# First loads of a fused attention and FFN kernel in 2 KB rows, split by partitions, with a third centred tile and a new hand-written order

## The chip, the cores and the metric

The kernel runs on one core of a Trainium2 chip. The metric is the device time of one execution in microseconds (us), the median of several runs. A core has five engines that run at the same time: TensorE (PE) for matrix products, VectorE (DVE), ScalarE (ACT), GpSimd (POOL) and SyncE (SP). SP and ACT also issue the transfers (DMAs) between the main memory and the on-chip memory. Each engine works through its own queue in order and waits at semaphores for the others.

## The reference

The input is x with 2048 tokens of 512 numbers in bf16. It is normalised per token, and two branches read the normalised xn; both are added to x.

```python
def reference(A_x, A_wqkv, A_wo, B_x, B_w_gate, B_w_up, B_w_down):
    xn = _layernorm(A_x)                       # eps 1e-5, no weights
    # A: linear attention, 32 heads of 16, over all tokens (no mask)
    q, k, v = split(xn @ A_wqkv)
    phi = lambda t: jnp.where(t > 0, t + 1, jnp.exp(t)) + 1e-6
    kv  = jnp.einsum("bhsd,bhse->bhde", phi(k), v)
    z   = jnp.einsum("bhsd->bhd", phi(k))
    o   = (phi(q) @ kv) / (phi(q) @ z + 1e-6)
    # B: gated FFN, 1792 wide
    return A_x + o @ A_wo + (silu(xn @ B_w_gate) * (xn @ B_w_up)) @ B_w_down
```

The sums over tokens in kv and z do not depend on the order of the tokens.

## The kernel before, in words

The 2048 tokens are 16 tiles of 128 tokens (tokens on the 128 partitions). The program is recorded by `_Program`: each step names its engine, what it reads and what it writes, and the class places the semaphores. The order in which steps are recorded is the order of every engine's queue; nothing is scheduled at run time. For the first part that order is written out by hand as a text of words in `run("""...""")`, one letter for the step and a number for the tile. `U0` and `U1` are the first two blocks of the FFN; a loop records the rest behind them.

The letters that matter here, with the lines of the profile before:

- `S` statistics of a tile on DVE: `bn1` (L257) and `bn2` (L263); tile 0 in two halves, `bnhalf` (L260) and `stat0`. `R` is `rs` on ACT (L272, L274): reciprocal standard deviation by Ln and Exp; `r` adds three powers of it (L279 to L281).
- `L` (`lna_dve`, L335) and `P` (`lna_pool`, L350 and L353) write the normalised tile xn on DVE or POOL.
- A centred tile goes another way: only the mean is subtracted before the projections, and the standard deviation is put in later as a scale inside Exp (L421) and as limits (`o`, `floor`, L284 and L287). `a` and `b` centre the halves of tile 0 (L297); `M` is the negative mean on ACT (`neg_mean`, L292) and `C` centring with it (L307); `J` (`xg_pool`, L327 and L330) writes the scaled tile that the sums over tokens need. The tiles in `CENTRED` are 0 and 1. Their xn is written later for the FFN alone.
- `c`, `d`, `W`, `X` are transposes on PE (`transp`, L365) of tiles 0 to 3; `e`, `g`, `h`, `v`, `w`, `Y` copy the result out of PSUM on ACT (L373) or DVE (L375). All other transposes are `D`, DMA transposes from SP (L381).
- `K` and `Q` are the projections of a tile (`proj`, L403), four products of 128x512 over the four chunks of the weight; `K0:3` is chunk 3 alone. `x` and `y` are their Exp on ACT (`phi_exp`, L421 centred, L424 otherwise), `m` and `n` the limits on POOL (`phi_min`, L431), `s` and `u` the sums on DVE (`phi_sum`, L442), which also free the PSUM banks. `G` (`gacc`, L452) adds a tile into the sums over tokens; these use banks 0 to 3, the projections mostly banks 4 to 7 in turn.
- `F1` is a filler product of 256 columns on PE (`keep_busy`, L247); seven of 512 columns stand ahead of all.
- `l` is a load of a later x tile from SP; `T0` to `T7` are the large weight loads from SP (0 and 4 the gate halves, 1 and 5 the up halves, 2 the value weights, 3 `wo`, 6 and 7 `wd`).

The first loads stand ahead of the text, on two queues: `("sp", "h00 K0 Q0 Q3 Q2 K1")` and `("act", "h01 x2 x3 Q1 x1 K3 K2")`. `h00` and `h01` are the column halves of x tile 0; each `K` or `Q` word is one 128x512 chunk of the weight, in rows of 1 KB.

The FFN (`gu`, L508; `hop`, L521), the output products (L638, L642) and the stores (L648 to L651) follow. `z_add`, `divide` and `scale_turn` compute the denominators beside them.

Of the kernel before, what the change touches and what calls it, by code (L numbers as in the profile page):

```python
# [9 lines left out]
P = 128  # L10
S = 2048
D = 512
F = 1792
NT = S // P
NCH = S // 512
NG = D // P
NDC = D // P
# [3 lines left out]
HPG = P // DH  # L21
NH = D // DH

CENTRED = (0, 1)
NC = len(CENTRED)
HALVED = (0,)
LOWBANK = {(1, 2): 0, (0, 2): 1}
NWARM = 7
O_SLOT = {5: 0, 8: 1, 11: 2, 13: 3}
# [79 lines left out]


def bass_parallel_sum__linear_attn_block__swiglu_ffn__prompt_kernel(nc, A_x, A_wqkv, A_wo, B_x, B_w_gate, B_w_up, B_w_down, out):
    xin = A_x[0]
    oview = out[0]
    K = _Program()
    bf, f32 = dt.bfloat16, dt.float32

    with contextlib.ExitStack() as es:
# [5 lines left out]
        x_sb = sb("x_sb", [P, NT, D], bf)  # L123
        xn = sb("xn", [P, NT, D], bf)
        r2 = sb("r2", [P, NC], f32)
# [7 lines left out]
        wqkv = sb("wqkv", [P, NDC, 3 * D], bf)  # L133
# [18 lines left out]
        out_sb = sb("out_sb", [P, 2, D], bf)  # L152
# [6 lines left out]
        stats = sb("stats", [P, NT + 1, 6], f32)  # L159
        mv = sb("mv", [P, NT, 2], f32)  # L160
# [7 lines left out]
        zt = pz[:, 0, :]  # L168
        shared = {(1, t): [("xc", t, 0), ("xc", t, 1)] for t in CENTRED}
        shared.update({(1, NC + t): [("xg", t)] for t in CENTRED})  # L170
        shared.update({(1, 2 * NC + a): [("xcT", t, h) for t in CENTRED for h in (0, 1)] for a in CENTRED})
        shared[1, 3 * NC] = [("junk",)]
# [5 lines left out]
        def B(i):  # L178
            return ("bank", i)


        def load(eng, key, dst, src):
            K.add(eng, lambda e: e.dma_start(dst, src), w=[key], dma=True)

        def xload(eng, t):
            load(eng, ("x", t), x_sb[:, t, :], xin[t * P:(t + 1) * P, :])

        def wload(eng, i, h=0, n=1):
            cs = slice(h * NDC // n, (h + 1) * NDC // n)
# [19 lines left out]
        K.add("act", lambda e: e.preload_act_table_set("natural_log_exp_and_others"))  # L209
        H = D // 2  # L210

        def xhalf(eng, t, h):
            load(eng, ("x", t, h), x_sb[:, t, h * H:(h + 1) * H], xin[t * P:(t + 1) * P, h * H:(h + 1) * H])

        def wchunk(eng, i, c):
            load(eng, ("wqk", i, c), wqkv[:, c, i * D:(i + 1) * D], A_wqkv[c * P:(c + 1) * P, i * D:(i + 1) * D])

        for eng, text in (("sp", "h00 K0 Q0 Q3 Q2 K1"),
                          ("act", "h01 x2 x3 Q1 x1 K3 K2")):
            for w in text.split():  # L220
                if w[0] == "h":
                    xhalf(eng, int(w[1:-1]), int(w[-1]))
                elif w[0] == "x":
                    xload(eng, int(w[1:]))
                else:
                    wchunk(eng, int(w[0] == "K"), int(w[1:]))

        K.add("pool", lambda e: e.memset(eps5[:, :], 1e-5), w=[("eps5",)])
        K.add("pool", lambda e: e.memset(ident[:, :], 0.0), w=[("ident",)])
# [1 line left out]
            out=ident[:, :], in_=ident[:, :], compare_op=ALU.not_equal, fill=1.0,  # L231
# [24 lines left out]
        def bn1(t):  # L256
            K.add("dve", lambda e: e.bn_stats(stats[:, t, :], x_sb[:, t, :]), r=xk(t), w=[("st", t)])  # L257

        def bnhalf(h):
            K.add("dve", lambda e: e.bn_stats(stats[:, h * NT, :], x_sb[:, 0, h * H:(h + 1) * H]), r=[("x", 0, h)], w=[("st", h * NT)])  # L260

        def bn2(t):
            K.add("dve", lambda e: e.bn_aggr(mv[:, t, :], stats[:, t, :]), r=[("st", t)], w=[("mv", t)])  # L263

        def stat0():
            bnhalf(0)
            bnhalf(1)
            K.add("dve", lambda e: e.bn_aggr(mv[:, 0, :], stats[:, 0::NT, :]), r=[("st", 0), ("st", NT)], w=[("mv", 0)])

        def rs(t):  # L270
            sl = slice(t, t + 1)
# [105 lines left out]
        def xkeys(t):  # L377
            return [("xnT", t)]
# [14 lines left out]
        def proj(i, t, cs):  # L393
            if (i, t) not in at:
                at[i, t] = LOWBANK[i, t] if (i, t) in LOWBANK else nextbank()
                begun[i, t] = 0
            b, col = at[i, t], i * D
            src = xcT if t in CENTRED else xnT
            fns = []
            for c in cs:  # L400
                first, last = begun[i, t] == 0, begun[i, t] == NDC - 1
                begun[i, t] += 1
                fns.append(lambda e, c=c, first=first, last=last: e.matmul(  # L403
                    banks[b][:, :], src[:, c, t * P:(t + 1) * P], wqkv[:, c, col:col + D], start=first, stop=last))
            keys = sorted({("xcT", t, c // 2) for c in cs}) if t in CENTRED else xkeys(t)
            K.add("pe", fns, r=keys + [("wqk", i, c) for c in cs], w=[B(b)])

        def efslot(b):
            return b - 4 if b >= 4 else b + 4
# [5 lines left out]
        def phi_exp(i, t):  # L415
            b = at[i, t]
            buf, bkey = ef[:, efslot(b), :], ("ef", efslot(b))
            if i == 0 and t in later:
                buf, bkey = pq[:, t, :], ("pq", t)
            if t in CENTRED:  # L420
                K.add("act", lambda e: e.activation(buf, banks[b][:, :], ACT.Exp, bias=lstd[:, t:t + 1], scale=rstd[:, t:t + 1]),  # L421
                      r=[B(b), ("rs", t), ("lstd", t)], w=[bkey])
            else:
                K.add("act", lambda e: e.activation(buf, banks[b][:, :], ACT.Exp), r=[B(b)], w=[bkey])  # L424

        def phi_min(i, t):
            buf, bkey = ef[:, efslot(at[i, t]), :], ("ef", efslot(at[i, t]))
            if i == 0 and t in later:
                buf, bkey = pq[:, t, :], ("pq", t)
            top, tkeys = (cap[:, t:t + 1], [("cap", t)]) if t in CENTRED else (1.0 + 1e-6, [])  # L430
            K.add("pool", lambda e: e.tensor_scalar(  # L431
                out=buf, in0=buf, scalar1=top, scalar2=0.0, op0=ALU.min, op1=ALU.max),
                r=[bkey] + tkeys, w=[bkey])

        def phi_sum(i, t):
            b = at[i, t]
            dst, dkey = ((pk[:, t, :], ("pk", t)) if i else (pq[:, t, :], ("pq", t)))
            low, lkeys = (flo[:, t:t + 1], [("flo", t)]) if t in CENTRED else (1e-6, [])
            val, mid, keys = banks[b][:, :], ef[:, efslot(b), :], [B(b), ("ef", efslot(b))]
            if i == 0 and t in later:  # L440
                val, mid, keys = tq[later[t]], pq[:, t, :], [("tq", later[t]), ("pq", t)]
            K.add("dve", lambda e: e.scalar_tensor_tensor(  # L442
                out=dst, in0=val, scalar=low, in1=mid, op0=ALU.max, op1=ALU.add),
                r=keys + lkeys, w=[dkey])
# [31 lines left out]
                  r=[fkey, ("pk", t)], w=[key])  # L476

        def stat(t):
            if t == 0:
                stat0()  # L480
                return
            bn1(t)
            bn2(t)

# [6 lines left out]
            "h": lambda t: evac(t, 2 * t + 1, "act", 2, 4), "f": lambda t: evac(t, 2 * t + 1, "dve", 2, 4),  # L491
            "W": lambda t: transp(t, 2), "v": lambda t: evac(t, 2, "act"), "w": lambda t: evac(t, 2, "dve"),
            "X": lambda t: transp(t, 3), "Y": lambda t: evac(t, 3, "act"), "Z": lambda t: evac(t, 3, "dve"),
            "l": lambda t: xload("sp", t), "K": lambda t, cs=range(NDC): proj(1, t, cs), "x": lambda t: phi_exp(1, t), "m": lambda t: phi_min(1, t), "s": lambda t: phi_sum(1, t),
            "Q": lambda t, cs=range(NDC): proj(0, t, cs), "y": lambda t: phi_exp(0, t), "z": phi_keep, "n": lambda t: phi_min(0, t), "u": lambda t: phi_sum(0, t), "G": gacc, "F": lambda t: keep_busy(t, 256),
        }

# [40 lines left out]
        def run(text):  # L538
# [5 lines left out]
                steps[k](t) if cs is None else steps[k](t, cs)  # L544

        run("""
            F1 F1 F1 S0 a0 R0 l9 c0 F1 r0 l13 F1 S2 J0 F1 g0 F1 b0 Q0:0 d0 R2 K0:0 h0 F1 o0 L2 W2 Q0:3 S3 v2 l4
            F1 R3 M1 P3 l11 Q0:1 F1 l6 Q0:2 y0 K2:0 Q2 S1 K0:3 C1 n0 S9 R1 T1 X3 l15 W1 K0:1 K0:2 r1 K2:1 K2:23
            l14 v1 y2 x0 K1 J1 Y3 S13 l5 u0 x2 o1 Q1 x1 m0 R13 S4 n2 m2 y1 P13 s0 K3 u2 m1 s2 x3 S15 m3 R4 Q3 R9
            y3 G2 s1 n1 G0 L4 s3 l10 l7 P9 l8 n3 G1 S5 D13 G3 u1 K13 P1 D4 S10 u3 Q13 R5 P5 D9 R15 x13 K4 m13  # L550
            y13 x4 n13 m4 S11 s13 u13 Q4 y4 G13 R10 D5 R11 K9 L15 D15 Q9 s4 x9 n4 l12 S7 R7 K5 m9 u4 L10 s9 Q5
            x5 S8 S14 G9 D10 P7 y9 m5 R8 P11 y5 n9 G4 D7 K15 x15 s5 n5 R14 S6 u9 L8 G5 K10 S12 D11 R6 u5 L6 m15
            s15 L14 K7 x10 Q11 x7 y11 D8 m10 K11 s10 D6 R12 m7 x11 s7 n11 L12 m11 Q10 y10 u11 Q8 s11 D14 K6 n10
            x6 P0 G11 D1 G7 u10 y8 m6 K8 K14 n8 u8 D12 x8 T2 m8 x14 K12 x12 s6 T5 s8 Q7 T0 D0 y7 m14 m12 G6 s14
            Q14 s12 Q6 n7 G12 Q12 y14 T3 y6 u7 Q15 G14 y12 y15 n12 n6 T4 G10 n14 u6 G8 u12 n15 u15 u14 U0 U1 T6
            G15 T7
        """)

        def gt_evac(c, eng):
# [87 lines left out]
        def oout(bank, t, lo, hi):  # L647
            K.add("dve", lambda e: e.tensor_tensor(  # L648
                out=out_sb[:, t % 2, lo:hi], in0=banks[bank][:, 0:hi - lo], in1=x_sb[:, t, lo:hi], op=ALU.add),
                r=[B(bank)] + xk(t), w=[("ob", t % 2, lo)])  # L650
            K.add("sp", lambda e: e.dma_start(oview[t * P:(t + 1) * P, lo:hi], out_sb[:, t % 2, lo:hi]),  # L651
                  r=[("ob", t % 2, lo)], w=[("out", t, lo)], dma=True)

        def otile(t):
# [86 lines left out]
```

## Time and profile before

| | us |
|---|---|
| runs shown | 213.12, 213.49, 213.58 |
| median | 213.49 |
| profiled execution, its own time | 213.12 |
| its span (first to last instruction) | 211.9 |
| PE busy | 207.9 |
| DVE busy | 122.9 |
| ACT busy | 67.4 |
| POOL busy | 66.7 |

The page cuts the span in 40 slices and gives the busy share of each engine in tenths. The chain that ended last goes back from the last instruction, step by step, to whatever released it. The stretches give busy time and count of instructions for PE, its weight loads, DVE, ACT and POOL, then the granted clock of PE, the share of the DMA engines and the GB/s. In a timeline an instruction's start and length are given; neighbours on one engine overlap by some 0.1 us, so the step from start to start is what an instruction costs its queue. The granted TensorE clock is 1.000 on average.

### The profile page before, as it was taken

The page shows a single profiled execution, that of the slowest core. Times are in us where ns is not written, and L with a number is a line of the kernel's source. Part 1 is how long each engine was busy: PE and PEld are TensorE (multiplying, and loading weights), DVE is VectorE, ACT ScalarE, POOL GpSimd, SP SyncE. Part 2 cuts the span into 40 slices and gives each one's busy share as a digit, 9 for nine tenths or more (in the row PEclk, how much of TensorE's full clock was granted, in tenths as well). Part 3 has the DMA queues.
Part 4 walks back from the last instruction along what each step waited for, and adds up shares of the span by engine and source line. Part 5 has one row for each costly group of instructions (what it writes and reads, how often), then busy time and mean ns, then how long its engine had stood idle before and what let it go on. Part 6 is the DMA issues. An engine that isn't in the chain of part 4 may idle for free.

```text
span 211.9 us, 2728 instructions
## 1 busy us (share of the span) xinstructions
PE 207.9 (98%) x998; PEld 96.9 (46%) x1017; DVE 122.9 (58%) x225; ACT 67.4 (32%) x140; POOL 66.7 (31%) x93
## 2 busy tenths in 40 slices
PE   8999999999999999999999999999999999999996
PEld 3534444444544444444444444444444444444445
DVE  4799997626984459454634674455447463625122
ACT  4794766462445333131221322120223131220000
POOL 3599667539960073202112022202202210000000
DMA  5963444899301101120101110111001122011101
GB/s 162 366 217 78 89 88 99 291 339 357 105 0 25 53 0 25 25 53 25 25 25 25 50 29 25 25 38 36 28 25 25 25 51 53 0 50 25 50 28 50
DMA packets 28349, 16.30 MB, mean 77 GB/s; under 512 B 18096, under 2 KB 28208, under 8 KB 28336
## 3 DMA queue, kind: packets, MB, share of 16 engines
q1 hardware_dynamic: 27328, 15.28, 25.7%
q10 hardware_dynamic: 1008, 0.85, 1.2%
q8 instruction: 8, 0.13, 0.3%
q14 instruction: 5, 0.04, 0.1%
HBM read 9.96 MB, written 2.10 MB: 57 GB/s over the span
## 4 chain that ended last, share of the span: by engine, by line
PE 93%; POOL 2%; ACT 1%; DVE 1%; issue 1%; POOLq 0%
PE pb L508 45%; PE pb L642 23%; PE pb L403 10%; PE pb L638 7%; PE pb L452 5%; PE pb L247 2%; POOL ef L431 1%; DVE pk L442 1%; PE pb L566 0%; PE pb L632 0%; POOL xn L353 0%; POOL hT L330 0%; ACT ef L421 0%; PE pb L365 0%; ACT hT L292 0%
## 5 line engine op out<-in xcount | busy, mean ns | idle before, releaser
L516 ACT ACTIVATE sil<-pb 128x512 bf16<-128x512 f32 x56 | 33.4, 597 | 103.8 <-PE pb L508 102.2
L521 DVE TENSOR_TENSOR hT<-pb,sil 128x512 bf16<-128x512 f32 x56 | 38.2, 683 | 38.7 <-PE pb L508 37.3
L508 PE MATMUL pb<-xnT,wu 128*128 128x512 bf16 x224 | 57.8, 379 | 0.0
L508 PE MATMUL pb<-xnT,wg 128*128 128x512 bf16 x214 | 55.8, 379 | 0.5
L642 PE MATMUL pb<-wd,hT 128*128 128x512 bf16 (+2 forms) x248 | 51.0, 355 | 0.2
L599 POOL TENSOR_TENSOR pz<-pq,zbc 128x512 f32<-128x512 bf16 x16 | 22.3, 1394 | 91.0 <-DVE den L606 78.5
L642 PEld LDWEIGHTS pb<-wd,hT 128*128 128x128 bf16 x252 | 23.5, 98 | 25.0
L508 PEld LDWEIGHTS pb<-xnT,wu 128*128 128x128 bf16 x224 | 21.9, 98 | 26.0
L508 PEld LDWEIGHTS pb<-xnT,wg 128*128 128x128 bf16 x224 | 21.8, 98 | 25.9 <-DVE pq L442 0.3
L648 DVE TENSOR_TENSOR out_sb<-pb,x_sb 128x512 bf16<-128x512 f32 (+2 forms) x18 | 11.4, 632 | 35.4 <-PE pb L642 35.4
L403 PE MATMUL pb<-wqkv,xnT 128*128 128x512 bf16 x111 | 25.8, 379 | 0.1
L431 POOL TENSOR_SCALAR ef<-ef 128x512 bf16<-128x512 bf16 x28 | 16.9, 612 | 10.4 <-ACT ef L424 10.3
L424 ACT ACTIVATE ef<-pb 128x512 bf16<-128x512 f32 x28 | 16.4, 594 | 10.6 <-PE pb L403 10.6
L403 PEld LDWEIGHTS pb<-wqkv,xnT 128*128 128x128 bf16 x112 | 10.8, 98 | 13.3 <-DVE pk L442 0.9
L638 PE MATMUL pb<-M,pk 128*128 128x512 bf16 (+2 forms) x71 | 16.7, 355 | 0.1
L452 PE MATMUL pb<-pk,xn 128*128 128x512 bf16 x54 | 13.6, 380 | 0.4 <-DVE pk L442 0.2
L442 DVE SCALAR_TENSOR_TENSOR pq<-pb,ef 128x512 bf16<-128x512 f32 x14 | 9.2, 678 | 6.1 <-POOL ef L431 6.0
L621 DVE TENSOR_TENSOR pq<-pq,rden 128x512 bf16<-128x512 bf16 x16 | 12.6, 787 | 0.0
L606 DVE TENSOR_REDUCE den<-pz 128x32 f32<-128x512 f32 x16 | 10.8, 675 | 0.0
L475 POOL TENSOR_TENSOR zacc<-zacc,pk 128x512 f32<-128x512 f32 x8 | 10.6, 1320 | 0.6
L257 DVE BATCH_NORM_STATS2 stats<-x_sb 128x6 f32<-128x512 bf16 x15 | 10.2, 679 | 0.6 <-DMA x_sb<-in_A_x_dram 0.6
L638 PEld LDWEIGHTS pb<-M,pk 128*128 128x128 bf16 x72 | 6.8, 98 | 7.4
(68 smaller groups left out, 107.4 us busy)
## 6 DMA issues: line engine op xcount, KB each, us to landing
out_dram<-out_sb SPq DMA_DIRECT2D x15, 128.0 KB, 1.7
wu<-in_B_w_up_dram SPq DMA_DIRECT2D x2, 896.0 KB, 6.4
wg<-in_B_w_gate_dram SPq DMA_DIRECT2D x2, 896.0 KB, 9.6
wd<-in_B_w_down_dram SPq DMA_DIRECT2D x2, 896.0 KB, 12.4
x_sb<-in_A_x_dram SPq DMA_DIRECT2D x12, 128.0 KB, 5.5
wqkv<-in_A_wqkv_dram SPq DMA_DIRECT2D x5, 128.0 KB, 4.0
wqkv<-in_A_wqkv_dram SPq DMA_DIRECT2D x1, 512.0 KB, 4.2
wo<-in_A_wo_dram SPq DMA_DIRECT2D x1, 512.0 KB, 7.9
```

The costliest lines, as they stand in the source:

```text
L403: fns.append(lambda e, c=c, first=first, last=last: e.matmul(banks[b][:, :], src[:, c, t * P:(t + 1) * P], wqkv[:, c, col:col + D], start= ...
L424: K.add("act", lambda e: e.activation(buf, banks[b][:, :], ACT.Exp), r=[B(b)], w=[bkey])
L431: K.add("pool", lambda e: e.tensor_scalar(out=buf, in0=buf, scalar1=top, scalar2=0.0, op0=ALU.min, op1=ALU.max), r=[bkey] + tkeys, w=[bkey])
L452: K.add("pe", [(lambda e, c=c: e.matmul(banks[c][:, :], src[:, t, c * P:(c + 1) * P], pk[:, t, :], start=first, stop=last)) for c in range ...
L508: fns.append(lambda e, c=c, b=b, w_=w_: e.matmul(banks[b][:, :], w_[:, c, fc * P:(fc + 1) * P], xnT[:, c, C * 512:(C + 1) * 512], start=(c ...
L516: K.add("act", lambda e: e.activation(sil[:, j % 2, :], banks[gb(j)][:, :], ACT.Silu), r=[B(gb(j))], w=[("sil", j % 2)])
L521: K.add("dve", lambda e: e.tensor_tensor(out=hT[:, C % 2, fc, :], in0=banks[gb(j) + 1][:, :], in1=sil[:, j % 2, :], op=ALU.mult), r=[B(gb( ...
L599: K.add("pool", lambda e: e.tensor_tensor(out=pz[:, t % 2, :].rearrange("q (g p) -> q g p", g=NG), in0=pq[:, t, :].rearrange("q (g p) -> q ...
L621: K.add("dve", lambda e: e.tensor_tensor(out=heads(pq[:, t, :]), in0=heads(pq[:, t, :]), in1=rden[:, i, :][:, :, None].broadcast_to([P, NH ...
L638: fns = [(lambda e, g=g: e.matmul(banks[bank][:, 0:hi - lo], pk[:, t, g * P:(g + 1) * P], M[:, g, lo:hi], start=(g == 0), stop=False)) for ...
L642: fns = [(lambda e, fc=fc: e.matmul(banks[bank][:, 0:hi - lo], hT[:, C % 2, fc, jj * P:(jj + 1) * P], wd[:, fc, lo:hi], start=False, stop= ...
L648: K.add("dve", lambda e: e.tensor_tensor(out=out_sb[:, t % 2, lo:hi], in0=banks[bank][:, 0:hi - lo], in1=x_sb[:, t, lo:hi], op=ALU.add), r ...
```

## The change

- The tokens are dealt to tiles in another way: tile 2b + a holds the tokens 256b + 2p + a (p the partition), so that a pair of tiles is 2 KB of neighbouring memory on each partition. The stores use the same map.
- The first loads are six names (`p0 W0 p2 W3 W1 W2`), each in two DMAs by partitions: 0 to 63 on SP, 64 to 127 on ACT. `p0` is x tiles 0 and 1, `W0` chunk 0 of the Q and K weights side by side. Later x tiles are loaded in pairs (`V`).
- Tile 0's statistics are taken in one piece. Tile 2 is centred too, with the steps that follow from it (`M2 C2 r2 o2 J2`, its xn by `P2`, its DMA transpose `D2`).
- The order text is new, with seven `F1` in place of ten. `z_add` is not changed.

```diff
-CENTRED = (0, 1)
+CENTRED = (0, 1, 2)
-HALVED = (0,)
+HALVED = (0, 1, 2, 3)
...
-    xin = A_x[0]
-    oview = out[0]
+    xin = A_x[0].rearrange("(b p a) d -> b p a d", p=P, a=2)
+    oview = out[0].rearrange("(b p a) d -> b p a d", p=P, a=2)
...
-        for eng, text in (("sp", "h00 K0 Q0 Q3 Q2 K1"),
-                          ("act", "h01 x2 x3 Q1 x1 K3 K2")):
...
+        HP = P // 2
+
+        def early(eng, ph, name):
+            i, ps = int(name[1:]), slice(ph * HP, (ph + 1) * HP)
+            if name[0] == "p":
+                load(eng, [("x", i, ph), ("x", i + 1, ph)], x_sb[ps, i:i + 2, :].rearrange("p a d -> p (a d)"),
+                     xin[i // 2][ps].rearrange("p a d -> p (a d)"))
...
+            elif name[0] == "W":
+                load(eng, [("wqk", 0, i, ph), ("wqk", 1, i, ph)], wqkv[ps, i, 0:2 * D],
+                     A_wqkv[i * P + ph * HP:i * P + (ph + 1) * HP, 0:2 * D])
...
+        for name in "p0 W0 p2 W3 W1 W2".split():
+            early("sp", 0, name)
+            early("act", 1, name)
+
+        def xpair(eng, t):
+            load(eng, [("x", t), ("x", t + 1)], x_sb[:, t:t + 2, :].rearrange("p a d -> p (a d)"),
+                 xin[t // 2].rearrange("p a d -> p (a d)"))
...
-            K.add("pe", fns, r=keys + [("wqk", i, c) for c in cs], w=[B(b)])
+            K.add("pe", fns, r=keys + [("wqk", i, c, ph) for c in cs for ph in (0, 1)], w=[B(b)])
...
         def stat(t):
-            if t == 0:
-                stat0()
-                return
             bn1(t)
             bn2(t)
...
-            F1 F1 F1 S0 a0 R0 l9 c0 F1 r0 l13 F1 S2 J0 F1 g0 F1 b0 Q0:0 d0 R2 K0:0 h0 F1 o0 L2 W2 Q0:3 S3 v2 l4
-            F1 R3 M1 P3 l11 Q0:1 F1 l6 Q0:2 y0 K2:0 Q2 S1 K0:3 C1 n0 S9 R1 T1 X3 l15 W1 K0:1 K0:2 r1 K2:1 K2:23
-            l14 v1 y2 x0 K1 J1 Y3 S13 l5 u0 x2 o1 Q1 x1 m0 R13 S4 n2 m2 y1 P13 s0 K3 u2 m1 s2 x3 S15 m3 R4 Q3 R9
-            y3 G2 s1 n1 G0 L4 s3 l10 l7 P9 l8 n3 G1 S5 D13 G3 u1 K13 P1 D4 S10 u3 Q13 R5 P5 D9 R15 x13 K4 m13
...
-            Q14 s12 Q6 n7 G12 Q12 y14 T3 y6 u7 Q15 G14 y12 y15 n12 n6 T4 G10 n14 u6 G8 u12 n15 u15 u14 U0 U1 T6
-            G15 T7
+            F1 V4 S0 F1 F1 F1 a0 M1 R0 c0 r0 F1 b0 C1 e0 S1 d0 W1 S2 K0:0 F1 h0 o0 F1 P0 Q0:0 v1 K0:3 V12 Q0:3
+            J0 M2 K1:03 R1 C2 r1 K0:1 S3 R2 W2 K1:1 r2 K0:2 o1 J2 V14 R3 Q0:1 Q0:2 w2 Q2 o2 x0 L3 m0 y0 X3 Y3 S5
+            n0 K2 y2 K1:2 K3:01 S13 s0 K3:23 x2 V10 R5 x1 n2 m2 Q3 u0 u2 x3 V6 y3 s2 R13 Q1 P5 y1 G0 m3 T0 V8 m1
+            J1 n1 n3 S4 s3 G2 G3 R4 L4 D5 s1 G1 L13 K5 x5 m5 S14 R14 D4 u3 u1 S8 R8 Q5 y5 D13 P8 L14 K4 s5 S6 Q4
+            G5 D14 x4 n5 u5 y4 D8 K13 Q13 R6 m4 n4 x13 s4 S9 u4 y13 K14 m13 G4 S15 R9 x14 n13 s13 T5 K8 L6 u13
...
+            Q6 y6 P10 s15 G6 n6 K7 Q15 D11 x7 K11 T2 u6 Q7 y15 m7 x11 m11 D2 n15 L1 y7 D10 G15 n7 G12 s7 u15 s11
+            Q11 Q9 D1 K10 u7 Q10 G9 x10 m10 y10 y11 n10 y9 s10 G7 T1 n9 T6 n11 G10 G11 T3 T7 u10 u11 u9 U0 U1 T4
...
-            K.add("sp", lambda e: e.dma_start(oview[t * P:(t + 1) * P, lo:hi], out_sb[:, t % 2, lo:hi]),
+            K.add("sp", lambda e: e.dma_start(oview[t // 2, :, t % 2, lo:hi], out_sb[:, t % 2, lo:hi]),
```

## The prediction

> **What bounds the kernel now.** I read the page's busy table and slices first, then the chain that ended last, then the timeline of the first 18 us engine by engine, the transfers, and the stretches.
>
> ```profile
> PE 207.9 (98%) x998; PEld 96.9 (46%) x1017; DVE 122.9 (58%) x225; ACT 67.4 (32%) x140; POOL 66.7 (31%) x93
> DVE  4799997626984459454634674455447463625122
> ```
>
> PE is the bound, and it does the same products after the change. So only the time in which PE does no product counts. The chain shows where that lies (start, length, engine, line):
>
> ```profile
> 0.84 3.79 PE pb L247 x10
> 4.62 0.21 PE pb L365 x2
> 4.84 0.85 PE pb L247 x4
> 5.69 0.43 PE pb L403
> 6.12 0.20 PE pb L365 x2
> 6.32 0.22 PE pb L403
> ...
> 16.58 0.61 DVE pk L442
> 17.23 1.04 PE pb L452 x4
> 18.27 3.45 PE pb L403 x16
> ```
>
> Until 5.69 PE runs fillers (L247). From 6.9 to 17.2 the chain wanders over ACT, POOL and DVE. The group at 17.23 is the last of the 48 first products (32 projections and 16 L452 products of tiles 0 to 3). From 18.27 on PE is full: at 3.45/16 = 0.216 us each, 48 products are 10.4 us and the 16 transposes under 1 us, so about 7 of the first 18.27 us are lost. Nothing else is to be won.
>
> The other engines in the stretches:
>
> ```profile
> 2.00:4.00 2.00, 2.00 (x7) 0.74 (x6) 1.08 (x4) 0.08 (x1) 0.53 (x3) 1.00 0.85 242
> 4.00:6.00 2.00, 2.00 (x11) 1.25 (x10) 1.76 (x6) 1.25 (x7) 1.01 (x2) 1.00 0.91 295
> 6.00:8.00 2.00, 2.00 (x16) 1.26 (x15) 1.33 (x4) 1.45 (x5) 0.57 (x3) 1.00 1.08 375
> 12.00:14.00 2.00, 2.00 (x10) 0.70 (x8) 1.72 (x4) 1.97 (x6) 1.86 (x5) 1.00 0.94 300
> 20.00:25.00 5.00, 4.95 (x23) 2.23 (x23) 4.93 (x12) 3.55 (x10) 3.34 (x7) 1.00 0.30 57
> ```
>
> Third to fifth busy columns: DVE, ACT, POOL; last: GB/s. ACT is full at 12 to 14, DVE at 20 to 25. ACT's steps, start to start, come from its timeline:
>
> ```profile
> 11.89 0.61 ACT L424 ACTIVATE ef<-pb 128x512 bf16<-128x512 f32 x1
> 12.36 0.80 ACT L421 ACTIVATE ef<-pb,lstd,rstd 128x512 bf16<-128x512 f32 x1
> 13.03 0.32 ACT L272 ACTIVATE lnv<-mv,eps 128x1 f32<-128x1 f32 x1
> 13.38 0.20 ACT L274 ACTIVATE rstd<-lnv 128x1 f32<-128x1 f32 x1
> 13.49 0.76 ACT L421 ACTIVATE ef<-pb,lstd,rstd 128x512 bf16<-128x512 f32 x1
> ```
>
> A plain exp or evacuation takes 0.48, a centred exp (L421) 0.66, the two steps of rs 0.45. The same reading gives 0.61 for neg_mean (7.82 to 8.43), 0.70 for rs with the three powers (9.09 to 9.79); on DVE 0.81 for a tile's statistics (17.10 to 17.91), 0.60 to 0.65 for phi_sum, 0.44 for centring, 0.32 to 0.60 for lna_dve; on POOL 0.65 for phi_min.
>
> **Part 1, the loads.** Before, x tile 0 came as two 64 KB halves, landed 2.0 and 2.2 us after issue (at 2.8 and 3.0). Now the first pair is 256 KB. The extra 131 kB at 375 to 242 GB/s cost 0.35 to 0.54, so it lands at 3.2 (the first half's landing plus the cheaper end) to 3.55; I take 3.3, near the fast end because nothing else is queued ahead. Summing the stretches, 1.07 MB had flowed by 6 and 1.82 MB by 8; the 786 kB up to tiles 2 and 3 flow by 5.0, all 1.57 MB by 7.3. Landings trailed the flow by 0.4 early and about 0.9 at 8, so tiles 2 and 3 land at 5.5, the last weights at 8.2. The first weight chunk lands at 4.5, before its use at 5.6. Tiles 2 and 3 are first wanted by DVE at 6.1; hidden. The last weights are wanted by ACT (through PE) at 8.9; hidden while ACT is full, 0.3 to 0.5 without that cover. The 2 KB rows may be faster than these 1 KB rows; no row shows it, and a gain there would be hidden too, except on the first pair (above: 3.2).
>
> The x loads of the later tiles go in pairs, 6 issues for 12 on SP, all issued before the first DMA transpose (14.55 before): nothing. Stores have the same sizes (1.7 us, behind DVE): nothing. The second gate half moves early, the first up half (wu) late, behind the transpose of tile 1. In the new order 15 groups of four products (0.86 each) lie between Q6 and the first gate product, 13 us. The transpose can issue 4 to 5.3 us after Q6 (phi of it, lna_dve, two transposes at 1.3 on SP), and wu landed in 6.0 to 6.7: at 12 by the worst, wanted at 13.8. Hidden; if the cover goes, at most 1 us.
>
> **Part 2, tile 2 centred.** It adds on ACT neg_mean 0.61 and powers 0.30, and turns two exps from 0.48 to 0.66 (0.36); ACT loses an evacuation of 0.48 to DVE. On DVE it adds centring 0.44 and that evacuation about 0.5, and drops an lna_dve of 0.5. On POOL it adds xg 1.05, floor 0.4, a later lna_pool 0.97; POOL is idle until exp comes and again after 30. One more DMA transpose, 1.3 on SP, lies in the 13 us above.
>
> **Part 3, the new order, walked.** DVE: statistics of tile 0 at 3.3, half centred at 4.25 (0.95 later, as 2.85 to 3.88 less the split's overhead), transposed at 4.75, so first product at 5.6 (5.69 before; 0.1 earlier). ACT: six issues end at 0.83 + 6 x 0.455 = 3.6; neg_mean of tile 1 to 4.2, rs and powers of tile 0 to 4.95, half evacuations 5.05 and 5.4, tile 1's at 5.9, neg_mean of tile 2 to 7.0, rs and powers of tiles 1 and 2 to 8.4, rs of tile 3 to 8.9. PE waits for tile 2's centring (7.1 to 7.55) and ends K0 by 8.3. Then ACT is full: x0, y0 to 10.2, evacuation of tile 3 to 10.7, y2, x2 to 12.0, rs 12.45, x1 13.1, x3, y3 14.1, rs 14.5, y1 15.2, rs of tile 4 to 15.6. DVE's lna of tile 4 waits for that: 15.7 to 16.3; s1, queued behind it, ends at 17.05; the products of tile 1, last of the 48, run 17.1 to 17.95.
>
> So the 48 products end at 17.95, where before PE began the next at 18.27: 0.32 less, bounds from the first landing (3.2 to 3.55) and the steps' spread (0.05 on some 15 ACT steps): minus 1.1 to plus 0.7. Behind it, PE per tile needs 12 x 0.216 = 2.59; DVE 0.81 + 1.2 + half an lna = 2.3. DVE walks on full, with phi_sums 0.3 to 0.8 ahead of the banks they free; one wait of 0.1 to 0.2 (s5 before its products). I book nothing for it. Sum: minus 0.3. Against the profiled execution (213.12, span 211.9 and 1.2 around it) that is 212.8; the median of the runs shown is 213.49, 0.37 above it, so the forecast is 213.2. A measurement of this kernel can tell about 0.2%, 0.43 us.
>
> **Rivals.** *The queues overlap better than my steps (faster).* For: after its first product the new order has two fillers, side by side, and then none; the old one had three, spread out to 7.34. If PE ran without a gap from the second product (5.9), 47 products and 8 transposes take 10.2 + 0.5: end 16.6, a gain of 1.7. Against: ACT is already full at 1.97 of 2. Between, 1.1: 212.4.
>
> *The clock rises late (slower).* Products before 6.12 take twice the time of those after (0.43 against 0.22), although the granted clock in the stretches reads 1.00: PE rose after 5.3 us of unbroken work. The new order's fillers (7 x 0.427 and 4 x 0.213) end at 4.7, and up to 5.6 PE has waits, 8 transposes and one filler. If the rise slips past W2, the seven products and two fillers before it go at 0.43 and 0.21: W2 at 9.4 for 7.85, x0 at 10.1 for 8.9, less the slack behind: plus 0.9, 214.4. It decides if PE is still at 0.43 after 6.5. The Trainium skill, "TensorE: Matmul & The Clock Gate" (Part 1: The HAM clock gate), says the clock doubles after one busy window of about 3.4 us in a free-running frame, and the same page (Part 4: PE-mode transpose) that transposes do not count as PE work in the same way; the trace agrees with a doubling, and no run here shows the frame. By that rule, as an estimate, a window spoiled after 4.7 leaves PE at half speed from about 6.1 to 9.5, which is the same 214.4.
>
> *DVE becomes the bound from 17 to 36 (slower).* At the same PE point the new order has about one statistics and one phi_sum more to do on DVE (1.2 us), and it is full already at 4.93 of 5. If lna_dve and phi_sum take their slow values (0.60, 0.65) throughout, 8 x 0.15 + 24 x 0.05 = 2.4 us, of which the margins of 0.3 to 0.8 and the 0.3 per tile take most: plus 0.7, 214.2. It decides where the waits show PE held by phi_sum after 20. Late loads would add to it. The Trainium skill, "SBUF — State Buffer" (Door 1: The DMA port swizzle), says that 64 neighbouring partitions reach only half of the 16 ports. By that, as an estimate, halves served one after the other would land the first pair 0.5 later, at 3.8, and add 0.3; no run here shows it, and in this order both halves are issued within 0.03 us of each other.
>
> **How the numbers follow.** Forecast 0.42 (its own range 212.4 to 214.2: faster by over 0.2% 0.14, within 0.24, slower 0.04); better overlap 0.20 (faster 0.19, within 0.01); late clock 0.16 (slower); DVE bound 0.22 (within 0.05, slower 0.17). Sums: 0.33, 0.30, 0.37. The range from 212.4 leaves out half of the overlap case, up to 214.7 the tails of the slow ones: 0.2 together.
>
> **What would show it.** First products at about 5.6, x0 at 8.9, ACT unbroken to 15.6, tile 1's L452-type products at 17.1, then a full PE. An x0 before 8.4 means the overlap case; 0.43 products after 6.5 the clock; waits of PE on phi_sum after 20 DVE. I am wrong if the first pair lands after 3.8, or if PE stalls before the first up product.

## The result, and the profile after

| | before | after |
|---|---|---|
| median of the runs | 213.31 | 215.14 |
| lowest and highest (4 runs each) | 213.12 to 213.58 | 214.91 to 215.67 |
| ratio of the runs (95%) | | 1.0095 (1.008 to 1.011) |
| profiled execution, its own time | 213.12 | 214.91 |
| its span | 211.9 | 213.4 |

With a fourth run (213.14) the median of the kernel before is 213.31. The change made the kernel 1.8 us slower (the quotient of the two medians is 1.0086, inside the interval). The forecast was 213.2 with a range of 212.4 to 214.7: the sign was wrong, and the range did not hold the time. The page of the profile after, busy table and slices:

```profile
PE 208.0 (97%) x995; PEld 96.3 (45%) x1014; DVE 124.5 (58%) x225; ACT 67.7 (32%) x145; POOL 68.2 (32%) x97
DVE  2799999636896459454645574545547463625122
```

PE is busy for as long as before; it stands still longer. Where, the chain that ended last says (start, length, engine, line; L404 are the projections, L453 the sums over tokens, L422 the centred exp):

```profile
1.42 0.87 ACTq L183
...
2.96 4.92 DMA wqkv<-in_A_wqkv_dram
...
7.98 1.40 PE pb L404 x5
...
12.18 1.34 ACT ef L422 x2
...
17.12 0.63 DVE xn L336
17.75 0.66 DVE pk L443
...
18.46 1.04 PE pb L453 x4
19.49 3.45 PE pb L404 x16
22.95 0.93 PE pb L453 x4
...
24.76 1.90 PE pb L404 x8
```

The chain before went through PE's own fillers and transposes up to 6.9. Now its front is a transfer: ACT's queue of DMA issues, and the fourth of them, a weight chunk, that PE waits for until 7.98. The last of the 48 first products start at 18.46 (17.23 before), the next product at 19.49 (18.27): 1.22 of the 1.5 us of span. Behind that point the kernel before needed 211.9 - 18.27 = 193.63 and the new one 213.4 - 19.49 = 193.91. That is 0.28 more, and the last and the third line from the end show most of it: eight products in 1.90 where eight without a gap take 1.73, four in 0.93 where they take 0.86. Outside the span lie about 1.5 us in place of 1.2. That difference holds in every run: time less span is 1.40 to 1.58 in the four of the new kernel and 1.22 to 1.30 in 19 of the kernel before. What these 0.3 are, the profile does not show. Of the kernels below, oldorder_split has 1.23 to 1.33 with the same loads, and mix 1.22 to 1.34 in nine of ten runs with the same order, so neither alone brings them.

The stretches (PE, its loads, DVE, ACT, POOL, clock, DMA share, GB/s):

```profile
2.00:4.00 2.00, 2.00 (x7) 0.74 (x6) 0.10 (x1) 0.08 (x1) 0.46 (x2) 1.00 0.71 192
4.00:6.00 2.00, 1.64 (x9) 0.78 (x7) 1.52 (x5) 0.98 (x4) 0.00 (x0) 1.00 1.04 311
6.00:8.00 2.00, 1.25 (x10) 0.59 (x10) 1.65 (x5) 2.00 (x10) 1.45 (x5) 1.00 0.88 279
20.00:25.00 5.00, 4.93 (x23) 1.99 (x23) 4.53 (x10) 3.55 (x11) 3.24 (x6) 1.00 0.33 67
```

The flow is 192 and 279 GB/s in the stretches from 2 and from 6 us where it was 242 and 375 (in between it is 311 where it was 295); the DMA engines are not idle for that, their share is 0.71 to 1.04. DVE did one operation from 2 to 4 where it had done four, and from 20 to 25 it is less full than before (4.53 against 4.93). ACT's timeline, first one issue of the kernel before, then the new kernel:

```profile
2.22 0.45 ACTq L183 DMA_DIRECT2D wqkv<-in_A_wqkv_dram  x1
```

```profile
0.83 0.56 ACTq L183 DMA_DIRECT2D x_sb<-in_A_x_dram  x1
1.42 0.87 ACTq L183 DMA_DIRECT2D wqkv<-in_A_wqkv_dram  x1
2.31 0.62 ACTq L183 DMA_DIRECT2D x_sb<-in_A_x_dram  x1
2.96 1.92 ACTq L183 DMA_DIRECT2D wqkv<-in_A_wqkv_dram  x3
4.99 0.63 ACT L293 ACTIVATE hT<-x_sb 128x512 bf16<-128x512 bf16 x1 [2.91 <-issue]
...
10.07 1.45 ACT L422 ACTIVATE ef<-pb,lstd,rstd 128x512 bf16<-128x512 f32 x2 [0.21 <-PE pb L404]
```

An issue of a 64-partition DMA holds ACT's queue for 0.56 to 0.87 us, where one of 128 partitions had held it for 0.40 to 0.46. The six end at 4.88, and neg_mean (L293), the first work of ACT, stands behind them. The first exp, x0, comes at 10.07.

### The profile page after: what moved, and what is told of

Read it like the earlier page. It is cut to its first block, busy times and chain, and to the rows that moved or that the text cites. A ratio compares the mean times of both kernels' runs of the same rounds, so it can differ in the third digit from the quotient of the medians.

```text
span 213.4 us, 2734 instructions
## 1 busy us (share of the span) xinstructions
PE 208.0 (97%) x995; PEld 96.3 (45%) x1014; DVE 124.5 (58%) x225; ACT 67.7 (32%) x145; POOL 68.2 (32%) x97
## 4 chain that ended last, share of the span: by engine, by line
PE 92%; ACT 3%; DMA 2%; DVE 1%; ACTq 1%; issue 1%
PE pb L506 45%; PE pb L639 23%; PE pb L404 11%; PE pb L635 6%; PE pb L453 5%; DMA wqkv<-in_A_wqkv_dram 2%; ACT ef L422 1%; ACTq L183 1%; ACT ef L425 0%; PE pb L563 0%; PE pb L629 0%; DVE pk L443 0%; DVE xn L336 0%; ACT rstd L275 0%; ACT xnT L374 0%
## 5 line engine op out<-in xcount | busy, mean ns | idle before, releaser
L404 PE MATMUL pb<-wqkv,xnT 128*128 128x512 bf16 x101 | 23.9, 379 | 0.2
L432 POOL TENSOR_SCALAR ef<-ef 128x512 bf16<-128x512 bf16 x26 | 15.8, 620 | 9.6 <-ACT ef L425 9.6
L425 ACT ACTIVATE ef<-pb 128x512 bf16<-128x512 f32 x26 | 14.8, 592 | 11.8 <-PE pb L404 11.7
L404 PEld LDWEIGHTS pb<-wqkv,xnT 128*128 128x128 bf16 x104 | 10.0, 98 | 12.7 <-DVE pq L443 0.8
L266 DVE BATCH_NORM_STATS2 stats<-x_sb 128x6 f32<-128x512 bf16 x16 | 10.9, 680 | 3.9 <-DMA x_sb<-in_A_x_dram 3.9
L453 PE MATMUL pb<-pk,xn 128*128 128x512 bf16 x52 | 12.7, 379 | 0.0
L443 DVE SCALAR_TENSOR_TENSOR pk<-pb,ef 128x512 bf16<-128x512 f32 x13 | 8.7, 678 | 2.9 <-POOL ef L432 2.9
```

The costliest lines, as they stand in the source:

```text
L404: fns.append(lambda e, c=c, first=first, last=last: e.matmul(banks[b][:, :], src[:, c, t * P:(t + 1) * P], wqkv[:, c, col:col + D], start= ...
L432: K.add("pool", lambda e: e.tensor_scalar(out=buf, in0=buf, scalar1=top, scalar2=0.0, op0=ALU.min, op1=ALU.max), r=[bkey] + tkeys, w=[bkey])
L443: K.add("dve", lambda e: e.scalar_tensor_tensor(out=dst, in0=val, scalar=low, in1=mid, op0=ALU.max, op1=ALU.add), r=keys + lkeys, w=[dkey])
L453: K.add("pe", [(lambda e, c=c: e.matmul(banks[c][:, :], src[:, t, c * P:(c + 1) * P], pk[:, t, :], start=first, stop=last)) for c in range ...
```

## The experiments

Two groups of theories. On the loads: ISSUE (ACT's queue is the loss), FLOW by rows, by place of the halves, or by their size, WEIGHTS (the new order needs weights earlier than they land). On the order: QUEUE (s1 stands behind the wait of tile 4 on DVE) and the order as such. The ratios are against the kernel before, run beside each group of kernels on the same chip (medians 213.07, 212.95 and 213.00; beside the change itself 213.31). So where times of different groups are set side by side, some 0.4 us is not to be read. 1 KB and 2 KB are the bytes per partition and row.

### New order with the old load shapes (neworder_1k)

```diff
-        for name in "p0 W0 p2 W3 W1 W2".split():
-            early("sp", 0, name)
-            early("act", 1, name)
+        for eng, text in (("sp", "h00 x1 K0 x2 K3 K1 K2"), ("act", "h01 Q0 x3 Q3 Q1 Q2")):
+            for w in text.split():
+                whole(eng, w)     # all 128 partitions; 1 KB rows, x tile 0 in two halves
```

> New order and tile 2 centred as in the change, but the first loads in 1 KB rows over all 128 partitions (x tile 0 in column halves, K and Q chunks apart), 7 DMAs on SP and 6 on ACT. Theory LOADS (the split 2 KB loads cost the time; the order is sound): DMA issues back at 0.43 to 0.46, neg_mean on ACT at 3.7, first product at 5.6, the 48 first products end near 18.0, time 213.0 to 213.4. Theory ORDER (the order and the third centred tile cost it): the 48 products still end after 19, time 214.5 or more.

Measured: 214.61, 1.0076 (1.0049 to 1.0103). The issues are back at 0.40 to 0.47, neg_mean at 3.76 and the first product at 5.70. But PE then waited 0.94 us for a weight chunk (until 7.46), x0's exp began at 9.39, and the product behind the 48 at 18.81. The old shapes did not bring the old time: with them too the new order waits for weights. The time is the one that ORDER named, the issues and the first product are those of LOADS, and the end of the 48 lies between the two: neither theory fits cleanly.

### Old order with the split loads (oldorder_split)

The kernel before with its own order and its two centred tiles, but the tokens dealt, the first loads made and tile 0's statistics taken in one piece as in the change:

```diff
-        for eng, text in (("sp", "h00 K0 Q0 Q3 Q2 K1"), ("act", "h01 x2 x3 Q1 x1 K3 K2")):
...
+        for name in "p0 W0 p2 W3 W1 W2".split():
+            early("sp", 0, name)
+            early("act", 1, name)
```

> The order and the two centred tiles of before, with the first loads of the change (split by partitions, 2 KB rows). Theory LOADS: first landing at 3.9 for 2.85 and last weights at 9.5, so the 48 products end 0.8 to 1.3 later than 18.27, time 214.2 to 214.7. Theory ORDER: 213.2 to 213.6.

Measured: 216.70, 1.0171 (1.0148 to 1.0193). The new loads cost the old order 3.6 us, far more than LOADS had allowed. PE waited for weights until 9.30 (0.84) and 10.05 (0.24); how much of that is the halves and how much that Q and K now come together, this kernel does not separate. With these loads the new order is better by 1.6 (215.14), with the old shapes it is worse by 1.5 (214.61 against 213.07). So the order alone is not the cause, nor are the loads alone: each costs time without the other.

### The same 2 KB rows, not split (whole2k)

```diff
+        for eng, text in (("sp", "p0 W3 W1"), ("act", "W0 p2 W2")):
+            for w in text.split():
+                whole(eng, w)     # 128 partitions, 2 KB rows, 256 KB each
```

> The change with the same 2 KB rows, but each name as one DMA over 128 partitions, three on each queue. Theory SPLIT (64-partition DMAs cost 0.57 to 0.63 a piece to issue and flow at 300 GB/s for 375): ACT is free at 2.7, the first pair lands near 3.6, all weights by 8.3, time 213.0 to 213.6. Theory ROWS (it is the 2 KB rows): weights land at 9 or later as in the change, time 214.5 or more. Theory ORDER: 214.5 or more with the weights early.

Measured: 214.33, 1.0059 (1.0042 to 1.0076), above the range of SPLIT and a little below that of the other two. One of its issues on ACT, and its stretches, columns as above:

```profile
1.25 0.46 ACTq L183 DMA_DIRECT2D x_sb<-in_A_x_dram  x1
```

```profile
2.00:4.00 2.00, 2.00 (x7) 0.74 (x6) 0.00 (x0) 0.08 (x1) 0.46 (x2) 1.00 0.98 321
4.00:6.00 2.00, 1.47 (x10) 0.86 (x9) 1.85 (x6) 1.67 (x8) 0.19 (x1) 1.00 1.04 383
6.00:8.00 2.00, 1.96 (x14) 0.97 (x12) 1.57 (x5) 1.93 (x7) 1.77 (x5) 1.00 1.04 387
```

The 2 KB rows are not the fault: whole, they flow at 321 to 387 GB/s, better than the 1 KB rows before. The split is, 0.8 us of it (the intervals of the two ratios do not overlap); the rest of the loss stays. The Trainium skill, "DMA: Bandwidth & Descriptors" (Rules for kernel authors), says of two transfers to disjoint halves of the partitions that they serialize, and advises one transfer of 128 partitions. The pair of runs agrees with the advice (215.14 split, 214.33 whole); that the halves serialize, no run here shows. The advice spoke against this change, and the prediction weighed halves served one after the other for the first pair of x alone. That pair is no argument against the halves, though: whole, it lands later (statistics at 4.08 against 3.90); that one queue carries it in one piece may be the reason, no run tests it. And PE still waited 0.50 for a weight.

### ACT with three issues only (actfree)

The last three names go whole on SP, so this kernel has fewer halves as well.

```diff
-        for name in "p0 W0 p2 W3 W1 W2".split():
+        for name in "p0 W0 p2".split():
             early("sp", 0, name)
             early("act", 1, name)
+        for name in "W3 W1 W2".split():
+            whole("sp", name)
```

> The change, but W3, W1 and W2 go as whole 256 KB DMAs on SP; ACT issues three halves and not six. Theory ISSUE (ACT's six issues until 4.9 hold back neg_mean): neg_mean starts when the first pair has landed, near 4.0, a gain of 0.7 to 1.0, time 214.0 to 214.4. Theory FLOW (late weights decide): K0:3 waits as before, gain below 0.3, time 214.8 or more.

Measured: 214.39, 1.0058 (1.0038 to 1.0078). Neg_mean moved from 4.99 to 3.87, but x0's exp only from 10.07 to 9.76: PE waited 0.62 and 0.27 for weights, at 7.39 and 8.68. The full ACT queue was one of two limits that ran side by side, and taking it away left the other. How much of the gain is the queue and how much the three whole loads, this kernel does not separate.

### Halves by even and odd partitions (evenodd)

```diff
-            i, ps = int(name[1:]), slice(ph * HP, (ph + 1) * HP)
+            i, ps = int(name[1:]), slice(ph, P, 2)
```

> The change with its halves as even and odd partitions (0, 2, 4 ... on SP; 1, 3, 5 ... on ACT); sizes, rows, counts and order unchanged. Theory PLACE (halves of neighbouring partitions crowd one half of the memory's ports): issues fall to 0.40 to 0.46, the loads flow at 370 to 390 GB/s in 4 to 8, no wait of PE on W3, time 214.2 to 214.5. Theory SIZE (64 rows or 128 KB a DMA is what costs): issues stay at 0.57 or more, 280 to 310 GB/s, 215.0 or more.

Measured: 215.28, 1.0106 (1.0089 to 1.0123). The first row is its stretch from 4 to 6, the second a row of its PE timeline:

```profile
4.00:6.00 2.00, 1.66 (x9) 0.79 (x7) 1.37 (x5) 0.98 (x4) 0.00 (x0) 1.00 0.89 278
```

```profile
7.56 2.58 PE L404 MATMUL pb<-wqkv,hT 128*128 128x512 bf16 x6
```

The issues cost what they did (0.56 to 0.87) and the flow stays low from 2 to 8: 246, 278, 271. That the 64 partitions are neighbours is not the cause. The other row shows six projections in 2.58, 0.43 each: in this execution PE was still at half speed until 9.98, where the profiled `after` had steps of 0.22 from 6.74 on. So the issues and the flow decide here, and not the time.

### Half a transfer, but twice the bytes (split256)

```diff
+            load(eng, [("x", t, ph) for t in range(4)], x_sb[ps, 0:4, :].rearrange("p (b a) d -> p b (a d)", a=2),
+                 xin[0:2, ps].rearrange("b p a d -> p b (a d)"))
+            for c0, c1 in ((0, 3), (1, 2)):
+                ...     # chunks c0 and c1 of Q and K in one DMA: 64 partitions, two rows of 2 KB
```

> The change with the same halves, but two names to a DMA (x tiles 0 to 3; W0 with W3; W1 with W2): 64 partitions, 128 rows of 2 KB, 256 KB each, three on each queue. One look at the loads; the first pair lands later by design. Theory SIZE (a DMA has a fixed price): 256 KB DMAs flow at 370 or more and issue at 0.46 or less as the whole ones do. Theory HALF (64 partitions are slower as such): 0.57 or more each, 300 GB/s.

One run: 218.4, span 216.9. Its time is not comparable, since x tile 0 comes with three others (statistics at 5.48). ACT's first issue:

```profile
0.83 0.71 ACTq L183 DMA_DIRECT2D x_sb<-in_A_x_dram  x1
```

Three DMAs of 256 KB per queue, as in whole2k, but over 64 partitions: issues of 0.61 to 0.84 where whole2k has 0.40 to 0.46, and a flow of 244, 221, 263 where it has 321, 383, 387. It is not a price per DMA of small size, either. What these experiments leave is the 64 partitions themselves; why they are slow stays open.

### s1 ahead of tile 4 on DVE (s1first)

In `after` DVE stood idle for 0.48 before tile 4's lna, and the sum of tile 1 was queued behind it (DVE's timeline):

```profile
17.12 0.63 DVE L336 TENSOR_SCALAR xn<-x_sb,mv,rstd 128x512 bf16<-128x512 bf16 x1 [0.48 <-ACT rstd L275]
17.67 0.73 DVE L443 SCALAR_TENSOR_TENSOR pk<-pb,flo,ef 128x512 bf16<-128x512 f32 x1
```

```diff
-            ... s3 G2 G3 R4 L4 D5 s1 G1 L13 K5 ...
+            ... s3 s1 G2 G3 G1 D5 R4 L4 L13 K5 ...
```

> The change with s1 (phi_sum of K of tile 1) and its products put ahead of tile 4's rs and lna; loads unchanged. Theory QUEUE (s1 stands ready at 16.6 but queues on DVE behind lna of tile 4, which waits for ACT until 17.1): the last of the 48 products start near 17.75 for 18.46, time 0.7 less, 214.3 to 214.6. Theory START (only the late start counts; later waits move on): gain below 0.25.

Measured: 214.64, 1.0086 (1.0064 to 1.0108), span 212.9 for 213.4. The wait of PE before these products (0.55) is gone, and the product behind the 48 starts at 18.87 for 19.49. The gain is 0.5 in the medians, and the two shorter spans of four are both 212.9 here and both 213.4 in `after`. The intervals of the two ratios overlap, though (1.0064 to 1.0108 and 1.008 to 1.011): the trace shows the queue, its price in time is less sure.

### Small x, whole weights, and both together (mix, mix_s1first)

```diff
+        for eng, text in (("sp", "x0 W0 W3 W2"), ("act", "x1 p2 W1")):
+            for w in text.split():
+                whole(eng, w)     # x0, x1: 128 partitions, 1 KB rows; the rest 2 KB rows
```

> The change's order, first loads over all partitions: x0 on SP and x1 on ACT in 1 KB rows, then 2 KB rows: W0, W3, W2 on SP, the pair p2 and W1 on ACT. Theory START: first landing near 3.1, neg_mean at 3.3, x0's exp at 8.7 to 9.0 and the last of the 48 products 8.4 later, 17.1 to 17.4; time 213.0 to 213.6. If the weights are not what holds x0's exp, it stays at 9.4 and the time at 214.3.

> Both edits of the two runs before. If they add: 212.3 to 212.9, below the kernel before. If each removes the same wait: as mix alone.

Measured: mix 213.77, 1.0041 (1.0024 to 1.0058); mix_s1first 213.95, 1.0047 (1.0032 to 1.0062). Mix has the issues, the early x (statistics 3.62) and the flow (321, 357, 347), and is 1.1 (by the ratios) to 1.4 (by the medians) better than `after`; PE still waited 0.88 for a weight, and x0's exp began at 9.34. With s1 moved as well nothing is added: x0's exp fell back to 9.81, ACT waiting 1.09 for PE, which had itself waited 1.02 and 0.27. The second of these waits is for a weight; the first the trace puts down to an ACT step, but the next kernel, which only does without the late chunks, does not have it. Of the two expected cases, adding up or the time of mix alone, the second came; the next kernel shows which wait is left. Mix's ten runs lie from 213.26 to 214.58, so the 0.2 between these two is not to be read.

### The weights not waited for (mix_s1_chunk0)

As mix_s1first, loads unchanged, but tiles 0 to 3 use weight chunk 0 in place of chunks 1 to 3, so that no early product waits for a late chunk:

```diff
-                    banks[b][:, :], src[:, c, t * P:(t + 1) * P], wqkv[:, c, col:col + D], start=first, stop=last))
+                    banks[b][:, :], src[:, c, t * P:(t + 1) * P], wqkv[:, c if t > 3 else 0, col:col + D], start=first, stop=last))
```

> As mix_s1first, but the projections of tiles 0 to 3 take weight chunk 0 for all four chunks, so that none waits for W1, W2 or W3 (their numbers are not the reference's); all loads go as before. Theory WEIGHTS (a projection is complete only with all the weights, 1 MB, and that sets x0's exp): PE's waits on weights vanish, x0's exp moves from 9.8 to 8.7, the 48 products end 1.0 earlier, 212.8 to 213.1. Theory ACT (ACT itself is late): x0's exp stays after 9.4, gain below 0.4.

So it computes other numbers than the reference; only its time is of use. Measured: 212.88, 0.9992 (0.9983 to 1.0001), a gain of 1.07 on mix_s1first. Of mix_s1first and then of this kernel, x0's exp on ACT and the chain where the 48 end (L420 are the projections):

```profile
9.81 1.45 ACT L438 ACTIVATE ef<-pb,lstd,rstd 128x512 bf16<-128x512 f32 x2 [1.09 <-PE pb L420]
...
18.52 3.45 PE pb L420 x16
```

```profile
8.99 1.43 ACT L438 ACTIVATE ef<-pb,lstd,rstd 128x512 bf16<-128x512 f32 x2
...
17.49 3.45 PE pb L420 x16
```

The end of the 48 moves by 1.03, so the 1.07 is the waiting for weights. With that gone, x0's exp begins at 8.99, where the prediction had it. But 17.49 is 0.78 ahead of the 18.27 before, and the time is no better than before: behind the 48 this kernel needs 211.6 - 17.49 = 194.1, 0.5 more than the old order.

### The K chunks first (kfirst, kfirst_s5)

The first exp needs the K products alone. So, starting from mix_s1first, the weights go in 1 KB rows, K ahead of Q, and the K products of tiles 0 and 1 go ahead of Q0:

```diff
-        for eng, text in (("sp", "x0 W0 W3 W2"), ("act", "x1 p2 W1")):
+        for eng, text in (("sp", "x0 K0 K3 K2 Q1 Q2"), ("act", "x1 p2 K1 Q0 Q3")):
...
-            ... F1 P0 Q0:0 v1 K0:3 V12 Q0:3 J0 M2 K1:03 ... V14 R3 Q0:1 Q0:2 w2 Q2 o2 x0 ... K1:2 K3:01 ...
+            ... F1 P0 v1 K0:3 V12 J0 M2 K1:03 ... V14 R3 K1:2 Q0 w2 Q2 o2 x0 ... K3:01 ...
```

> As mix_s1first, but the K chunks are loaded ahead of the Q chunks in 1 KB rows, and the order does tile 0's and tile 1's K products before tile 0's Q; banks as before. Theory WEIGHTS: half the weights (0.5 MB) are enough for x0's exp, which moves to 8.7 to 9.1; 212.8 to 213.3. If 1 KB rows flow so much slower that the K chunks land no earlier than 7.5: as mix_s1first, 213.9.

Measured: 213.49, 1.0021 (1.0011 to 1.003), the best of the new-order kernels with all weights in use. PE waits for no weight any more, x0's exp is at 9.13, the product behind the 48 at 18.12, 0.15 ahead of the kernel before. Behind the 48 it needs 212.1 - 18.12 = 194.0, 0.35 more than before.

This profiled execution is the slowest of the ten (213.65), and PE was at half speed in it until 6.7. The first row is its two fillers of 256 columns, 0.215 each from start to start; the second is one filler of the next kernel, kfirst_s5, which has the same order up to there and took 0.10 for it:

```profile
6.29 0.62 PE L272 MATMUL pb<-const-bfloat16-1.0 128*128 128x256 bf16 x2
```

```profile
4.96 0.27 PE L272 MATMUL pb<-const-bfloat16-1.0 128*128 128x256 bf16 x1
```

At full speed that early, kfirst_s5 has x0's exp at 8.66 and the product behind the 48 at 17.65. Two of kfirst's ten runs took 213.0, the other eight 213.3 to 213.7; whether the speed of PE at the start is what parts them is not shown.

To win back the 0.35, kfirst_s5 moves one word, s5 ahead of tile 8's statistics, where the chain had shown PE waiting for a sum:

```diff
-            ... D4 u3 u1 S8 R8 Q5 y5 D13 P8 L14 K4 s5 S6 Q4
+            ... D4 u3 u1 s5 S8 R8 Q5 y5 D13 P8 L14 K4 S6 Q4
```

> As kfirst, and s5 goes ahead of tile 8's statistics and tile 14's lna on DVE. If the waits of PE behind tile 4's Q (about 0.07 and 0.17 before s5's products and the K products of tile 13) come from that queue, 0.1 to 0.25 less than kfirst; otherwise the same.

Measured: 214.40, 1.0069 (1.0052 to 1.0085), a miss. The one long wait of PE, for a sum (L459) that frees the bank of a projection (in total, times, longest):

```profile
PE pb L420 <- DVE pq L459: 1.4, 1, 1.4
```

On DVE s5 now waits for its exp and limit until 19.88 and holds back the statistics of tile 8; ACT, POOL and the sum u5 follow from these, and PE stands for 1.4 us until 24.3.

## Why the prediction was wrong

| step | forecast | after |
|---|---|---|
| first x tile at DVE | 3.3 | 3.90 |
| ACT's issues end | 3.6 | 4.88 |
| first product | 5.6 | 6.74 |
| x0's exp | 8.9 | 10.07 |
| last of the 48 start | 17.1 | 18.46 |

- **What failed first: the durations of the loads (Part 1).** The prediction took issue time (0.455) and flow (242 to 375) from rows of DMAs over 128 partitions. The halves cost 0.56 to 0.87 to issue, and flowed at 192 to 311: ACT's queue was free at 4.88 for 3.6, and PE waited for a weight until 7.98. The condition that it named for being wrong, a first pair after 3.8, came true. For that pair the halves are not to blame, since whole it landed at 4.08: there the sum of the old landing and 131 kB of flow was too short, for a whole 256 KB as for two halves. The prediction's sentence on halves from the Trainium skill, "SBUF — State Buffer" (Door 1: The DMA port swizzle), had given 3.8 as an estimate, which is near the 3.90; but evenodd, whose halves are not neighbours, flows no faster, so the trace does not bear out that reason, and the near number is luck. The prediction put 0.3 on it, as an addition to another rival; against whole2k the halves cost 0.8.
- **"Hidden while ACT is full" failed as a step of its own.** It compared the landing of the last weights (8.2) with the exp (8.9), and booked at most 0.5 without the cover. But PE needs the chunks one after the other before that exp. In the old order Q's four chunks and one of K, 0.66 MB, stood before the first exp; in the change all four double chunks W0 to W3, 1 MB, and 0.5 MB of x must be there. ACT was not covered by other work at that time: it stood idle for PE before x0, 0.21 in `after` and 1.09 in mix_s1first, where its queue of issues is short. The cost, measured alone on mix_s1first, is 1.07.
- **The sum compared unlike things.** It set 17.1 + 0.86 = 17.95 against 18.27, which is 17.23 + 1.04. Like with like it is 17.1 + 1.04 = 18.14 against 18.27: a gain of 0.13 where the text has 0.32.
- **Behind the 48, "I book nothing" was 0.28.** All new-order kernels worked out above give back 0.3 to 0.5 there. The one wait that the text names, for s5, was the right kind (in `after` 0.07 before its products, and 0.17 among the projections behind them), and moving s5, the obvious cure, made it worse.
- **What was right:** the walk from x0's exp to the last products of the 48, 8.2 forecast and 8.39 measured; s1 queued behind tile 4; the first product at 5.6 and x0 at 8.9, in the kernels that have the early landings (5.70 in neworder_1k, 8.99 in mix_s1_chunk0). The half loads of the FFN weights, the later pairs and the stores cost nothing that the chain shows.
- **The rivals.** Better overlap did not occur; even without a wait for weights the 48 ended only 0.78 earlier, where that rival had 1.1 to 1.7. The late clock did not occur in the profiled execution (steps of 0.22 from 6.74), but evenodd, split256 and, up to 6.7, kfirst have it, so it was a real risk, and which executions it takes is not settled here. DVE as the bound did not occur: it is 4.53 of 5 from 20 to 25. "Late loads would add to it" was the sentence that came true, and it stood as a side remark, not as a rival with a price.

The terms, against the 212.8 forecast for the profiled execution (214.91, so 2.11 more): x0's exp late 1.17, the walk behind it 0.19, the comparison 0.19, behind the 48 0.28, outside the span 0.3; together 2.13. The first is the loads and the weights, which the experiments split. The 0.3 outside the span is open.

Why the change does not pay is then in two runs. With the loads repaired as far as was found here and s1 moved, the new order reaches 213.49 (213.0 in two runs of ten). With no weight to wait for at all it reaches 212.88, which is the time before. So no more than the time before was to be had in these variants of the new order; what the change loses beyond that lies in its first loads, the halves (0.8) and the weights that come late for this order, and to a part that the times do not settle in the place of s1.

## What to carry to other kernels

When a load changes shape, take its issue time and its flow from rows of that shape, and where there is none, treat both as unknown, with a range that includes half the flow. When an order changes, list which bytes must have landed before the first step of the engine that sets the pace, and not only when each transfer lands. Where two limits run side by side, as the full ACT queue and the late weights did, removing one shows only its lead over the other: test them together, and then each out of that.

## What the runs showed of the hardware

- Among the first loads, a DMA over 64 partitions from SP or ACT took 0.56 to 0.87 us to issue, one over 128 partitions with one row each 0.40 to 0.47, at equal bytes too (256 KB: 0.61 to 0.84 in split256, with two rows to a partition, against 0.40 to 0.46 in whole2k).
- The same bytes in the same 2 KB rows flowed at 321 to 387 GB/s from 2 to 8 us in whole DMAs (whole2k), and at 192 to 311 in halves on two queues (`after`), with the DMA engines 0.98 to 1.04 and 0.71 to 1.04 busy. Interleaved halves were no better (246 to 278, evenodd).
- The moment at which PE goes from 0.43 to 0.22 us per product moved between about 4 us (mix, whose first eleven fillers take 3.46 where those of `after` take 4.00), 6 us (before) and 10 us (evenodd), with the granted clock at 1.00 in the stretches of all three; in split256, where PE stood longer at the start (0.84 busy of 2 from 4 to 6), products still took 0.43 up to 11.9.
